# Moving one attention output piece per period by one dense product

## The chip, the cores and the metric

The kernel runs on one core of a Trainium2 chip. The metric is the device time of one execution in microseconds (us), as the median of several runs. TensorE does the matrix products; VectorE, ScalarE and GpSimd empty the PSUM banks, take exponentials and mask; SyncE issues most of the DMA transfers.

## The reference

A transformer block with a pre-norm attention over a sliding window of 256 keys and a dense part with SiLU, for 2048 rows of width 1024, 32 heads of width 32 and a hidden width of 3584:

```python
qkv = layernorm(x) @ wqkv                       # 3 x 32 heads x 32
scores = einsum("bhqd,bhkd->bhqk", q, k) * 32 ** -0.5
mask = (i - j >= 0) & (i - j < 256)
p = softmax(where(mask, scores, -1e9))
h = x + einsum("bhqk,bhkd->bhqd", p, v) @ wo
out = h + silu(layernorm(h) @ w1) @ w2
```

## The kernel before

The 2048 rows are worked in four blocks of 512. TensorE runs one stream of dense products, 128x128 weights against 512 columns, in groups of eight that add up in one PSUM bank: first the q, k and v products of all blocks (lines 252 and 262), then the output projection of the attention (line 283), then the two matrices of the dense part (lines 728 and 756). Three banks (`bank0` to `bank2`) serve the groups in turn; after each group VectorE copies or adds the bank out (lines 254, 264, 285).

Attention is woven into this stream by the class `Attention`. Its counter `seen` counts dense products, and `between` is called ahead of each product: when the counter has reached a number in `pieces` or `visits`, that piece of attention work is put into TensorE's order there. The numbers are written out by hand. `i` counts units of four heads of one block; i = 0 to 7 (block 0) are done with `scores_0`, and the other 24 units in twelve periods of two units each. Period p starts at product t = 256 + 48p and has:

- three score visits, at t + 4, t + 20 and t + 36. A visit (`visit`, line 360) multiplies q and k for 36 to 48 small tiles. Its own tiles go into the four-bank tile `sc`, and, since that is not enough room, others go into the dense bank that is idle, the dense bank of the group just finished ("behind"), and the output bank `bank3`. The products are sorted by column, so that the first 24 of a visit write `sc`, and those for the other banks follow. A product that writes the bank "behind" has to stand after VectorE's copy of that bank. ScalarE then takes the exponentials (lines 315, 321, 322), and GpSimd masks (line 409).
- four output pieces (`attn_piece`), each 24 products of probabilities with v into the output bank `bank3` (line 419), followed by `attn_norm` on VectorE: a reciprocal of the sums (line 430) and a multiply that reads the output bank and writes `obuf` (line 431). Two pieces (heads 0 and 1, then 2 and 3) make a unit; after the second one a transposing DMA of `obuf` is put on the list `late`, which is run, on SyncE's queue, ahead of the next dense group (line 439).

There is one output bank, so a piece must wait until the norm of the piece before has read it, and a visit that uses it must do so too. The first visit of the next period stands at t + 52. Groups of eight start at multiples of eight, so products t + 40 to t + 47 make one group.

Of the kernel before, what the change touches and what calls it, by code (L numbers as in the profile page):

```python
# [47 lines left out]
def kernel(  # L48
# [328 lines left out]
    def scores_0(g, odd):  # L377

        q0 = odd * P
        parts = [  # L380
            (odd, 0, q0, q0 + 320, 0), (odd, 1, q0, q0 + 384, 0),
            (odd + 2, 0, q0 + 256, 448, 320), (odd + 2, 1, q0 + 320, 448, 384),
        ]
        if odd:
            parts = [(a, h, f, min(t, 512), c) for a, h, f, t, c in parts[:2]] + [
                (3, 0, 384, 512, 320), (3, 1, 448, 512, 384), (2, 0, 448, 512, 448), (2, 1, 448, 512, 448)]
        for step in range(0, len(parts), 2):
            for hh in range(4):
                for t, half, qa, qb, col in parts[step:step + 2]:
                    r0 = hh * DH  # L390
                    k0 = t * P + half * 64
                    nc.tensor.matmul(  # L392
                        sc[half * 64:half * 64 + 64, hh, col:col + qb - qa],
                        lhsT=kT[0][r0:r0 + DH, g, k0:k0 + 64],
                        rhs=qT[0][r0:r0 + DH, g, qa:qb],
                        start=True, stop=True, tile_position=(r0, half * 64),
                    )
        e = (ybuf if odd else xbuf)(g)[:, 0:2048].rearrange("p (h q) -> p h q", q=512)
        nc.scalar.activation(out=e[:, :, 0:256], in_=sc[:, :, 0:256], func=ACT.Exp, scale=scale)  # L399
        nc.scalar.activation(out=e[:, :, 320:512], in_=sc[:, :, 256:448], func=ACT.Exp, scale=scale)  # L400
        nc.scalar.activation(out=c_ring[:, (g + 1) % 3, :, 128 + 64 * odd:192 + 64 * odd], in_=sc[:, :, 448:512],
                             func=ACT.Exp, scale=scale)
        select(e[:, :, 0:P], e[:, :, 0:P], True)
        select(e[:, :, 256:384], e[:, :, 320:448], False)
        select(e[:, :, 384:512], e[:, :, 384:512], True)
# [42 lines left out]
    class Attention:  # L448


        def __init__(self):
            self.seen = 0
            self.visits, self.pieces = {}, {}
            for d in range(2 * G):
                self.visits[92 + 10 * d] = lambda d=d: scores_0(d // 2, d % 2)
                self.pieces[(122 + 10 * d, 267, 284)[max(d - 13, 0)]] = (d // 2, d % 2)
            for p in range((NB - 1) * G // 2):
                i, t = G + 2 * p, 256 + 48 * p
                for n in range(3):
                    self.visits[t + 4 + 16 * n] = lambda i=i, n=n: visit(i, n)  # L460
                for n in range(4):
                    self.pieces[t + (41, 45, 59, 76)[n]] = (i + n // 2, n % 2)

        def between(self, kt):
            if self.seen in self.pieces:
# [168 lines left out]
    for g0 in range(0, G, 4):  # L634
        for w in range(2):
            for g in range(g0, g0 + 4):
                run_late()
                n = g0 * 2 + w * 4 + g % 4
# [170 lines left out]
```

## Time and profile before

| what | value |
|---|---|
| median of 3 runs | 690.12 us (689.69 to 690.25) |
| profiled execution | 690.01 us |
| its span, first to last instruction | 688.3 us |
| mean granted TensorE clock | 1.000 |
| TensorE matmul (PE) busy | 674.4 us, 98% |
| TensorE weight load (PEld) busy | 338.1 us, 49% |
| VectorE (DVE) busy | 296.0 us, 43% |
| ScalarE (ACT) busy | 237.8 us, 35% |
| GpSimd (POOL) busy | 155.4 us, 23% |
| attention periods p = 0 to 11 | about 99 to 270 us |

A row of the profile gives an engine, a line of the kernel, an operation with the tile that it writes and the tiles that it reads, and a count; in a timeline the first column is the start and the second the duration, and an idle time of the engine ahead of the row stands in brackets with what ended it. PE rows are matmuls, PEld rows are the weight loads ahead of them. The matmuls are pipelined, so a row's duration reaches beyond the start of the next one, and a few matmul records are missing from the trace; the weight loads are all there.

### The profile page before, as it was taken

The page shows a single profiled execution, that of the slowest core. Times are in us where ns is not written, and L with a number is a line of the kernel's source. Part 1 is how long each engine was busy: PE and PEld are TensorE (multiplying, and loading weights), DVE is VectorE, ACT ScalarE, POOL GpSimd, SP SyncE. Part 2 cuts the span into 40 slices and gives each one's busy share as a digit, 9 for nine tenths or more (in the row PEclk, how much of TensorE's full clock was granted, in tenths as well). Part 3 has the DMA queues.
Part 4 walks back from the last instruction along what each step waited for, and adds up shares of the span by engine and source line. Part 5 has one row for each costly group of instructions (what it writes and reads, how often), then busy time and mean ns, then how long its engine had stood idle before and what let it go on. Part 6 is the DMA issues. An engine that isn't in the chain of part 4 may idle for free.

```text
span 688.3 us, 14482 instructions
## 1 busy us (share of the span) xinstructions
PE 674.4 (98%) x6099; PEld 338.1 (49%) x6200; DVE 296.0 (43%) x616; ACT 237.8 (35%) x412; POOL 155.4 (23%) x247
## 2 busy tenths in 40 slices
PE   9999999999999999999999999999999999999998
PEld 4445555555555555444444444444444444444445
DVE  5287745774444446733316133343233251333111
ACT  7356666666767664023300033300133100233000
POOL 1046656666676665000000000000000000000000
DMA  8823144124522687765023310023300124100110
GB/s 274 260 53 96 21 59 101 26 42 106 174 78 71 199 283 212 157 244 202 1 87 112 84 39 1 0 92 73 81 1 0 31 87 90 39 1 0 31 38 24
DMA packets 77617, 61.50 MB, mean 89 GB/s; under 512 B 52464, under 2 KB 60656, under 8 KB 77552
## 3 DMA queue, kind: packets, MB, share of 16 engines
q1 hardware_dynamic: 77408, 60.31, 31.3%
q8 instruction: 48, 0.79, 0.5%
q10 hardware_dynamic: 144, 0.26, 0.1%
q14 instruction: 17, 0.14, 0.1%
HBM read 39.85 MB, written 8.39 MB: 70 GB/s over the span
## 4 chain that ended last, share of the span: by engine, by line
PE 97%; issue 2%; DMA 1%; DVE 0%; SPq 0%; ACT 0%; ACTq 0%; DVEq 0%
PE hacc L728 16%; PE bank L262 16%; PE hacc L756 15%; PE bank L756 13%; PE bank L728 12%; PE bank L283 8%; PE bank L252 6%; PE bank L419 5%; PE sc L360 2%; PE bank L360 1%; PE bank L547 1%; PE sc L392 1%; DMA r_w<-in_A_wqkv_dram 1%; PE tp L252 1%; ACT r_e L321 0%
## 5 line engine op out<-in xcount | busy, mean ns | idle before, releaser
L409 POOL TENSOR_SCALAR_AFFINE_SELECT r_e<-r_e 128x512 bf16<-128x512 bf16 x240 | 152.5, 643 | 115.3 <-ACT r_e L399 52.4
L756 PEld LDWEIGHTS <-r_a 128*128 128x128 bf16 x952 | 90.9, 98 | 103.0
L728 PEld LDWEIGHTS <-r_w 128*128 128x128 bf16 x896 | 87.7, 98 | 105.7
L756 PE MATMUL hacc<-r_a 128*128 128x512 bf16 (+2 forms) x523 | 103.2, 356 | 0.5
L756 PE MATMUL bank<-r_a 128*128 128x512 bf16 x412 | 91.4, 379 | 0.5
L728 PE MATMUL hacc<-r_e,r_w 128*128 128x512 bf16 x375 | 84.4, 379 | 0.5
L262 PEld LDWEIGHTS <-r_w 128*128 128x128 bf16 x512 | 45.4, 97 | 49.3 <-issue 1.0
L728 PE MATMUL bank<-r_e,r_w 128*128 128x512 bf16 x284 | 63.9, 379 | 0.1
L264 DVE CAST r_a<-bank 128x512 bf16<-128x512 f32 x58 | 40.1, 691 | 53.9 <-PE bank L262 34.3
L262 PE MATMUL bank<-r_t,r_w 128*128 128x512 bf16 x236 | 57.1, 379 | 2.6 <-issue 2.2
L262 PE MATMUL bank<-r_w 128*128 128x512 bf16 x240 | 56.4, 379 | 1.9 <-issue 1.6
L283 PE MATMUL bank<-r_o,r_a 128*128 128x512 bf16 x242 | 56.4, 379 | 1.5 <-issue 1.1
L419 PEld LDWEIGHTS <-r_e 128*128 128x128 bf16 x1440 | 45.6, 96 | 16.8 <-issue 3.2
L321 ACT ACTIVATE r_e<-sc 128x1536 bf16<-128x1536 f32 x36 | 53.4, 1482 | 0.0
L737 ACT ACTIVATE r_n<-bank 128x512 f32<-128x512 f32 x18 | 10.7, 597 | 117.0 <-PE bank L728 117.0
L419 PE MATMUL bank<-r_a,r_e 128*128 128x33 bf16 x1440 | 46.2, 178 | 0.1
L315 ACT ACTIVATE r_e<-bank 128x512 bf16<-128x512 f32 x48 | 26.1, 597 | 45.0 <-PE bank L360 45.0
L737 ACT ACTIVATE r_n<-hacc 128x512 f32<-128x512 f32 x24 | 14.3, 597 | 75.5 <-PE hacc L728 74.3
L771 DVE SCALAR_TENSOR_TENSOR r_t<-bank,r_t 128x512 bf16<-128x512 f32 x15 | 10.3, 684 | 66.6 <-PE bank L756 66.6
L283 PEld LDWEIGHTS <-r_a 128*128 128x128 bf16 x256 | 23.4, 97 | 25.8
L771 DVE SCALAR_TENSOR_TENSOR r_t<-hacc,r_t 128x512 bf16<-128x512 f32 (+2 forms) x19 | 12.0, 632 | 53.1 <-PE hacc L756 53.1
L252 PE MATMUL bank<-r_w,r_t 128*128 128x512 bf16 x118 | 28.9, 379 | 1.1 <-issue 0.8
(100 smaller groups left out, 574.8 us busy)
## 6 DMA issues: line engine op xcount, KB each, us to landing
r_w<-in_B_w_dram SPq DMA_DIRECT2D x8, 896.0 KB, 6.0
r_a<-in_B_w_dram SPq DMA_DIRECT2D x7, 1024.0 KB, 9.8
r_w<-in_A_wqkv_dram SPq DMA_DIRECT2D x4, 1024.0 KB, 8.3
h_dram<-r_t SPq DMA_DIRECT2D x16, 256.0 KB, 2.8
r_t<-h_dram SPq DMA_DIRECT2D x16, 256.0 KB, 2.9
out_dram<-r_t SPq DMA_DIRECT2D x31, 128.0 KB, 1.7
r_e<-h_dram SPq DMA_DIRECT2D x3, 1024.0 KB, 5.8
r_o<-in_A_x_dram SPq DMA_DIRECT2D x11, 256.0 KB, 5.5
```

What stands on the lines that cost most here:

```text
L252: nc.tensor.matmul(acc, lhsT=lnT_b[b % 2][:, kt, j * P:(j + 1) * P], rhs=wv[:, kt, c * 512:(c + 1) * 512], start=(kt == 0), stop=(kt == KT ...
L262: nc.tensor.matmul(acc, lhsT=wqk[:, kt, col0:col0 + P], rhs=lnT_b[b % 2][:, kt, :], start=(kt == 0), stop=(kt == KT - 1))
L264: copy(out=(qT, kT)[which][b][:, g, :], in_=acc)
L283: nc.tensor.matmul(acc, lhsT=qT[b][:, g, j * P:(j + 1) * P], rhs=wo[:, g, c * 512:(c + 1) * 512], start=(g == 0), stop=(g == G - 1))
L315: nc.scalar.activation(out=c_ring[:, lo:hi + 1:hi - lo, h, :], in_=four[bank].rearrange("p (n q) -> p n q", q=256), func=ACT.Exp, scale=scale)
L321: nc.scalar.activation(out=tri_of(e)[:, h0:h1, :, 64:256], in_=tri, func=ACT.Exp, scale=scale)
L409: nc.gpsimd.affine_select(out=dst, in_=src, pattern=[[0, n] for n in dst.shape[1:-1]] + [[sgn, P]], compare_op=ALU.is_ge if upper else ALU ...
L419: nc.tensor.matmul(o_ps[:, qt * 2 + hh, 0:VW], lhsT=chunk_of(i, bank, piece, pair * 2 + hh), rhs=v[:, b * 4 + kt, g * 4 + pair * 2 + hh, : ...
L728: nc.tensor.matmul(acc, lhsT=w1[:, kt, ft * P:(ft + 1) * P], rhs=ln2T[b][:, kt, :], start=(kt == 0), stop=(kt == KT - 1))
L737: nc.scalar.activation(out=th, in_=acc, func=ACT.Tanh, scale=0.5)
L756: nc.tensor.matmul(acc[:, 0:c1 - c0], lhsT=gT[:, ft, j * P:(j + 1) * P], rhs=w2[ft // 4][:, ft % 4, c0:c1], start=(ft == 0), stop=(ft == F ...
L771: nc.vector.scalar_tensor_tensor(out=t_out[j % 2][:, c0:c1], in0=acc[:, 0:c1 - c0], scalar=0.5, in1=t_in[j % 2][:, c0:c1], op0=ALU.mult, o ...
```

## The change

The third visit of a period stands at t + 36, five products ahead of the first output piece at t + 41. The second piece stood at t + 45; it now stands at t + 46, still within the same dense group. Between the two pieces there are then five dense products in place of four, and between the second piece and the next period's first visit at t + 52 six in place of seven. Nothing else differs.

```diff
                 for n in range(4):
-                    self.pieces[t + (41, 45, 59, 76)[n]] = (i + n // 2, n % 2)
+                    self.pieces[t + (41, 46, 59, 76)[n]] = (i + n // 2, n % 2)
```

## The prediction

> **What bounds the kernel now.** I read the page first: its span, the busy shares, and the chain that ended last.
>
> ```profile
> span 688.3 us, 14482 instructions
> PE 674.4 (98%) x6099; PEld 338.1 (49%) x6200; DVE 296.0 (43%) x616; ACT 237.8 (35%) x412; POOL 155.4 (23%) x247
> PE 97%; issue 2%; DMA 1%; DVE 0%; SPq 0%; ACT 0%; ACTq 0%; DVEq 0%
> ```
>
> TensorE is busy 98% of the span and carries 97% of the chain. So time is won only where TensorE stands still or waits, and what is won there moves the end by as much, unless a later wait takes it back. The edit touches twelve places, the second output piece (line 419) of each of the twelve periods. I therefore asked next for the weight loads of that line over the stretch that holds these periods, with what they waited for.
>
> ```profile
> L419 PEld LDWEIGHTS <-r_e x1104: 95/96/98, 101.3 to 269.0; 128*128 128x128 bf16 x184
> its engine sat idle before it (us, times) until:
>   issue: 3.0, 12
> ```
>
> Twelve interruptions, one for each period, 3.0 us in all; the 1104 loads are 46 pieces of 24, and the other 34 (first, third, fourth) show none. Third came the timeline of one period, around the third visit's two pieces. Columns are start, duration, engine, line.
>
> ```profile
> 206.36 0.27 ACT L322 ACTIVATE r_e<-bank 128x128 bf16<-128x128 f32 x1
> 206.39 0.59 PE L262 MATMUL bank<-r_t,r_w 128*128 128x512 bf16 x2
> 206.61 0.86 PEld L419 LDWEIGHTS <-r_e 128*128 128x128 bf16 x24
> 206.82 0.76 PE L419 MATMUL bank<-r_a,r_e 128*128 128x33 bf16 x24
> 207.40 0.55 PEld L262 LDWEIGHTS <-r_w 128*128 128x128 bf16 x4
> 207.42 1.02 PE L262 MATMUL bank<-r_t,r_w 128*128 128x512 bf16 x4
> 207.68 0.21 DVE L430 RECIPROCAL recip<-bank 128x8 f32<-128x8 f32 x1
> 207.93 0.42 DVE L431 TENSOR_TENSOR r_n<-bank,recip 128x256 bf16<-128x256 f32 x1
> 208.07 0.10 PEld L419 LDWEIGHTS <-r_e 128*128 128x128 bf16 x1
> 208.40 0.75 PE L419 MATMUL bank<-r_a,r_e 128*128 128x33 bf16 x24
> 208.40 0.65 PEld L419 LDWEIGHTS <-r_e 128*128 128x128 bf16 x23 [0.24 <-issue]
> 208.98 1.20 PEld L262 LDWEIGHTS <-r_w 128*128 128x128 bf16 x7
> 209.19 0.21 DVE L430 RECIPROCAL recip<-bank 128x8 f32<-128x8 f32 x1 [0.84 <-PE bank L419]
> 209.43 0.42 DVE L431 TENSOR_TENSOR r_n<-bank,recip 128x256 bf16<-128x256 f32 x1
> 209.85 0.69 DVE L264 CAST r_a<-bank 128x512 bf16<-128x512 f32 x1
> 209.92 1.19 SPq L439 DMA_TRANSPOSE r_a<-r_n  x1
> 210.60 0.57 PEld L360 LDWEIGHTS <-r_a 32*64 32x64 bf16 x48 [0.42 <-issue]
> 210.60 0.43 PE L360 MATMUL sc<-r_a 32*64 32x320 bf16 x24
> 210.85 0.47 PE L360 MATMUL bank<-r_a 32*64 32x128 bf16 x24
> 211.32 1.57 ACT L315 ACTIVATE r_e<-bank 128x512 bf16<-128x512 f32 x3 [2.30 <-PE bank L360]
> ```
>
> Both pieces write the one output bank. The second may not write before VectorE's norm of the first (lines 430 and 431) has read it. The norm ends at 207.93 + 0.42 = 208.35 and the second piece's first matmul starts at 208.40, 0.05 later, while its first weights had been in since 208.17. That the norm is the releaser is borne out by the one period where it is late:
>
> ```profile
> 117.80 0.10 PEld L419 LDWEIGHTS <-r_e 128*128 128x128 bf16 x1
> 117.80 0.42 DVE L431 TENSOR_TENSOR r_n<-bank,recip 128x256 bf16<-128x256 f32 x1
> 118.28 0.65 PEld L419 LDWEIGHTS <-r_e 128*128 128x128 bf16 x23 [0.38 <-issue]
> 118.86 1.20 PEld L252 LDWEIGHTS <-r_w 128*128 128x128 bf16 x7
> 119.73 0.69 DVE L254 CAST r_a<-bank 128x512 bf16<-128x512 f32 x1
> 120.48 0.57 PEld L360 LDWEIGHTS <-r_a 32*64 32x64 bf16 x48 [0.42 <-issue]
> ```
>
> Here it ends at 118.22, and the piece goes on at 118.28, after 0.38 of idle instead of 0.24.
>
> **The change part by part.** No instruction is added, removed or resized; 24 matmuls with their weight loads, one reciprocal and one multiply per period come one dense product later in TensorE's order.
>
> *What goes.* A dense product takes 0.215 us: the row at 206.39 holds two in 0.59, that at 207.42 four in 1.02, so two more cost 0.43. Without a wait the second piece's first matmul would start one product after its first weight load, at 208.07 + 0.215 = 208.285; it starts 0.115 later. The whole slot says the same: from the piece's first weight load to the next product's it is 208.98 - 208.07 = 0.91, against 207.40 - 206.61 = 0.79 for the first piece, 0.12 more. In the late period the slot is 118.86 - 117.80 = 1.06, 0.27 more by these rounded rows. The group row makes the ordinary period general: 3.0 less the late one's 0.38, over eleven, is 0.24, the very idle of the period shown. So the stalls are worth 11 x 0.115 + 0.26 = 1.5 us.
>
> With one product more, the ordinary piece's natural start is 208.285 + 0.215 = 208.50, past the release at 208.40 by 0.10. A release that comes shortly ahead costs nothing: the first piece's bank is freed by ScalarE at 206.36 + 0.27 = 206.63, it starts at 206.82, and its slot is the 0.79. So the wait goes entirely in eleven periods. In the late one the natural start is 117.80 + 0.43 = 118.23 and the release 118.28: 0.05 stays. Gain 1.45 us. From below: if the piece's new place in its group of eight cost 10 ns each, and the 3.0 us stands rounded, 1.3; from above: by idle alone, 3.0 - 12 x 0.12 (the idle behind a first weight load that needs no wait: 0.215 less its 0.10) = 1.56, less the 0.05, 1.5.
>
> *What is late next.* The piece itself begins 0.10 later (208.50 for 208.40), and so does everything VectorE does behind it: reciprocal from 209.29, norm until 209.95, and queued behind the norm the cast of the finished dense group, 209.95 to 210.64. The dense products behind the piece, and with them the next period's first visit (line 360), come 0.115 earlier: the visit at 210.49, and its 24 products into the chained banks from 210.74 on. One of these banks is that which the cast empties, and in the order in which the code sorts the visit's products it is the fifth of the 24, about 210.75. The cast's release is 210.64 + 0.05 = 210.69. In the trace of before this cover is 210.86 - 210.59 = 0.27; it shrinks to some 0.06, and does not go. I cost it at nothing. The late period has as much: cast until 120.42, release 120.47, and its visit at 120.27, its bank products from 120.52. In the last period no visit follows.
>
> The output bank, which the same visit writes too, is free at 209.95 + 0.05, 0.7 ahead. SyncE's transpose of the normed tile waits for the norm: 0.10 later, its data are for the last projection, and it is issued at the same group boundary in SyncE's order, so no load is overtaken. ScalarE waits 2.30 for the visit at 211.32 and moves with it; GpSimd follows ScalarE.
>
> *Sum.* The profiled execution took 690.01 us with a span of 688.3; less 1.45 it is 688.56. The median of the three runs is 690.12, 0.11 above; carried over, 688.67, that is 0.21% less.
>
> **The rivals.** *The cover is too thin by the refill.* [...]
>
> ```profile
> 60.41 0.10 PEld L419 LDWEIGHTS <-r_e 128*128 128x128 bf16 x1
> 60.73 0.50 PEld L419 LDWEIGHTS <-r_e 128*128 128x128 bf16 x17 [0.22 <-issue]
> 61.26 0.32 PEld L392 LDWEIGHTS <-r_a 32*64 32x64 bf16 x24
> ```
>
> From 60.73 until about 61.48 (61.26 + 0.32 less a load of 0.10) 17 + 24 weight loads with their matmuls came: at most 18 ns a pair, and less if the array was the limit. At 18 ns the 20 pairs from the waiting product on would need until 210.69 + 0.36 = 211.05; their natural last load is 210.60 + 0.57 - 0.10 - 0.115 = 210.955. Loss 0.095 in eleven periods, 1.05 us: 689.7 at worst, nothing at 13 ns or below. I take 689.4 for this case. For it: the cover of 0.06. Against: visits show weight loads a few ns apart, and the 18 ns is a ceiling.
>
> [...]
>
> *Slower: the visit needs the cast at its head.* If what is held up by the cast were the visit's first product, not its 29th (one wait for the whole visit, or a queue that must be full before it starts), the release at 210.69 would stand against 210.49: 0.20 lost for 0.115 won, and a refill of 48 pairs at 18 ns, 0.86 for the visit's 0.50 or so, another 0.36. That is 0.445 net in ten periods and 0.35 in the late one, less 0.115 in the last: 4.7 us, 694.8; without the refill still 0.8, 690.9. It decides from the point where the release is needed ahead of 210.69, so anything that wants it 0.06 before its bank product tips toward it. For it: today the cast ends at 210.54, 0.06 ahead of the visit, so the trace of before would hide such a need. Against: the gap ahead of a visit (0.42) is the same in the late period, and the first 24 products write only the score tile.
>
> *Nothing moves.* The 0.12 could belong to a second piece as such, wherever it stands: 690.1. Against: the 0.38 that follows the late norm.
>
> **How the numbers follow.** A measurement of this kernel can tell about 0.2%, 1.4 us, from no change, so the forecast lies almost on that bound. The stall goes as worked out: 0.76. Of this 0.58 I put beyond 0.2% and 0.18 within, since the gain of 1.3 to 1.5 straddles 1.38, and the higher of its terms rest on the better rows. Thin cover: 0.08, within. Nothing moves: 0.05, within. Slower at the head: 0.11, of it 0.09 with the refill, over 0.2% slower, and 0.02 within. Faster 0.58, same 0.33, slower 0.09. The predicted time is 688.67. The range goes down to 688.2 (the 1.5, and the 0.43 by which the lowest run of before lies below its median) and up to 689.6, which takes in the thin cover's 689.4 and leaves out no change and the slower case, 0.16 together.
>
> **What would show it.** Right: the interruptions of line 419's weight loads in this stretch fall from twelve to one, of about 0.17; the second piece's slot falls to 0.79 or 0.80; reciprocal and norm of that piece stand one product later against the piece before; the gap ahead of the next first visit stays 0.42 and its 48 loads stay 0.57; the dense line's count between the two pieces is five, not four. Thin cover: the visit's loads stretch beyond 0.57 by up to 0.1. Slower: the 0.42 becomes 0.6 or more in eleven periods. Nothing moves: an idle of 0.24 stays ahead of the piece's second load. The prediction is wrong if TensorE's time ahead of the last projection does not shrink by 1.3 to 1.5 us, or if that gain is gone again by the end.

## The result

| kernel | median | runs | ratio to before, 95% interval |
|---|---|---|---|
| before | 689.99 us | 13 (689.68 to 690.45) | |
| changed | 688.79 us | 13 (688.25 to 690.04) | 0.9981 [0.9973, 0.9989] |

The change makes the kernel 1.20 us faster by the medians, 0.17%; the ratio in the table says 0.19%, and its interval ends below 1, so a gain is there, though a small one. The forecast was 688.67 in a range of 688.2 to 689.6. On the bound of 0.2% that the prediction set for itself the result falls just within, as its text said it might; it had given the larger chance, 0.58, to the other side.

The profiled execution of the changed kernel took 689.66 us with a span of 688.0. That is only 0.35 below the 690.01 of before, so its stages have to be read apart. First the page, then the weight loads of line 419 over the periods, with what they waited for:

```profile
span 688.0 us, 14583 instructions
PE 682.9 (99%) x6200; PEld 338.0 (49%) x6200; DVE 295.0 (43%) x616; ACT 237.8 (35%) x412; POOL 155.5 (23%) x247
PE 98%; DMA 1%; SPq 0%; DVE 0%; issue 0%
```

```profile
L419 PEld LDWEIGHTS <-r_e x1122: 95/96/98, 98.3 to 268.9; 128*128 128x128 bf16 x187
its engine sat idle before it (us, times) until:
  issue: 0.2, 1
```

Twelve interruptions have become one, and 3.0 us of idle 0.2. That is not 2.8 us won: in every piece, waiting or not, TensorE's weight loads stand still for 0.12 us behind the first one (in each of the 62 pieces of this trace without a wait; at 208.38 the first load takes 0.10 and the second starts at 208.60), which this view does not count, and that part stays. (The PE busy time is higher because this trace lacks no matmul records, 6200 for 6099.) The timeline of the same period as in the prediction:

```profile
207.49 0.77 PEld L262 LDWEIGHTS <-r_w 128*128 128x128 bf16 x5
207.52 1.24 PE L262 MATMUL bank<-r_t,r_w 128*128 128x512 bf16 x5
207.77 0.21 DVE L430 RECIPROCAL recip<-bank 128x8 f32<-128x8 f32 x1
208.02 0.42 DVE L431 TENSOR_TENSOR r_n<-bank,recip 128x256 bf16<-128x256 f32 x1
208.38 0.87 PEld L419 LDWEIGHTS <-r_e 128*128 128x128 bf16 x24
208.59 0.76 PE L419 MATMUL bank<-r_a,r_e 128*128 128x33 bf16 x24
209.17 0.98 PEld L262 LDWEIGHTS <-r_w 128*128 128x128 bf16 x6
209.39 0.21 DVE L430 RECIPROCAL recip<-bank 128x8 f32<-128x8 f32 x1 [0.94 <-PE bank L419]
209.63 0.42 DVE L431 TENSOR_TENSOR r_n<-bank,recip 128x256 bf16<-128x256 f32 x1
209.97 0.68 DVE L264 CAST r_a<-bank 128x512 bf16<-128x512 f32 x1
210.58 0.57 PEld L360 LDWEIGHTS <-r_a 32*64 32x64 bf16 x48 [0.42 <-issue]
210.83 0.47 PE L360 MATMUL bank<-r_a 32*64 32x128 bf16 x24
```

Five products stand between the pieces. The norm ends at 208.44, the piece starts at 208.59, its 24 weight loads run through in one group, and its slot is 209.17 - 208.38 = 0.79. The visit behind keeps its gap of 0.42 and its 0.57. The late period:

```profile
118.89 0.10 PEld L419 LDWEIGHTS <-r_e 128*128 128x128 bf16 x1
119.16 0.65 PEld L419 LDWEIGHTS <-r_e 128*128 128x128 bf16 x23 [0.17 <-issue]
119.73 0.98 PEld L252 LDWEIGHTS <-r_w 128*128 128x128 bf16 x6
```

Its slot is 0.84, 0.05 above the others; that is the one interruption left.

Where, then, are the other 1.1 us of this execution? At the start and at the end of the periods, neither of which the change touches. TensorE's third value product (line 547) started 0.62 us later, since it waited for value weights from DRAM. First the row of before, then that of the changed kernel:

```profile
6.65 5.93 PE L547 MATMUL bank<-r_w 128*128 128x512 bf16 x25 [0.28 <-DMA r_w<-in_A_wqkv_dram]
7.27 6.07 PE L547 MATMUL bank<-r_w 128*128 128x512 bf16 x26 [0.95 <-DMA r_w<-in_A_wqkv_dram]
```

And the last period's third visit was held up:

```profile
264.87 0.65 PEld L360 LDWEIGHTS <-r_a 32*64 32x64 bf16 x36 [0.42 <-issue]
265.58 0.76 PEld L283 LDWEIGHTS <-r_a 128*128 128x128 bf16 x5
```

By the time of the first score product of block 0 this execution was 0.99 us behind that of before (41.57 for 40.58, the first weight load of line 392), all of it lost in the first 22 us. The visit's slot is 265.58 - 264.87 = 0.71 where it was 0.58. Between the first load of line 392 and the first of line 728, the stretch that holds all the periods, the trace of before has 257.78 us and this one 256.44: 1.34 less, which is 1.47 less 0.13 at that visit; the slots of the twelve pieces account for 1.45 of the 1.47. So the gain is there in full, and what a single run shows of it depends on the start and on that visit. The experiments look into both.

### The profile page after: what moved, and what is told of

Same layout as the page of the kernel before. It is cut to its first block, busy times and chain, and to the rows that moved or that the text cites. A ratio compares the mean times of both kernels' runs of the same rounds, so it can differ in the third digit from the quotient of the medians.

```text
span 688.0 us, 14583 instructions
## 1 busy us (share of the span) xinstructions
PE 682.9 (99%) x6200; PEld 338.0 (49%) x6200; DVE 295.0 (43%) x616; ACT 237.8 (35%) x412; POOL 155.5 (23%) x247
## 4 chain that ended last, share of the span: by engine, by line
PE 98%; DMA 1%; SPq 0%; DVE 0%; issue 0%
PE bank L262 17%; PE hacc L728 16%; PE hacc L756 15%; PE bank L756 13%; PE bank L728 12%; PE bank L283 8%; PE bank L252 7%; PE bank L419 5%; PE sc L360 2%; DMA r_w<-in_A_wqkv_dram 1%; PE bank L360 1%; PE sc L392 1%; PE tp L252 1%; PE bank L547 0%; PE tp L499 0%; SPq L150 0%
## 5 line engine op out<-in xcount | busy, mean ns | idle before, releaser
L262 PE MATMUL bank<-r_t,r_w 128*128 128x512 bf16 x256 | 61.3, 379 | 0.0
L262 PE MATMUL bank<-r_w 128*128 128x512 bf16 x256 | 59.4, 379 | 0.1
L283 PE MATMUL bank<-r_o,r_a 128*128 128x512 bf16 x256 | 58.9, 379 | 0.0
L252 PE MATMUL bank<-r_w,r_t 128*128 128x512 bf16 x128 | 30.5, 380 | 0.0
```

What stands on the lines that cost most here:

```text
L252: nc.tensor.matmul(acc, lhsT=lnT_b[b % 2][:, kt, j * P:(j + 1) * P], rhs=wv[:, kt, c * 512:(c + 1) * 512], start=(kt == 0), stop=(kt == KT ...
L262: nc.tensor.matmul(acc, lhsT=wqk[:, kt, col0:col0 + P], rhs=lnT_b[b % 2][:, kt, :], start=(kt == 0), stop=(kt == KT - 1))
L283: nc.tensor.matmul(acc, lhsT=qT[b][:, g, j * P:(j + 1) * P], rhs=wo[:, g, c * 512:(c + 1) * 512], start=(g == 0), stop=(g == G - 1))
```

## The experiments

Theory: the second piece waits for the norm of the first; each product between them hides 0.215 us of it; and the visit behind needs VectorE's cast only at its 29th product. Rivals: the visit needs the cast at its head; the 0.12 us belong to any second piece; the change makes a later wait.

**One product more: t + 47.**

```diff
-                    self.pieces[t + (41, 46, 59, 76)[n]] = (i + n // 2, n % 2)
+                    self.pieces[t + (41, 47, 59, 76)[n]] = (i + n // 2, n % 2)
```

> Own theory (the second piece waits for the norm, and the next visit needs the bank behind only at its 29th product): no wait left at the piece, its slot 0.795 us in all twelve periods. The norm of the second piece ends 0.215 us later than at t + 46, so the cast's release comes some 0.16 us after the visit's 29th product would start. The visit's weight loads stretch from 0.57 to about 0.73 us in eleven periods, 1.75 us lost for 1.50 won against before: 690.2 us, up to 691.5 if the refill behind the wait takes 18 ns a pair. The gap ahead of the visit stays 0.42. Rival (the visit needs the cast at its head): the gap grows by about 0.42 us to 0.84 in eleven periods, 693 us or more. Rival (the cover is never used): 688.5 us.

Measured: 689.32 us, ratio 0.9985 [0.9976, 0.9994]. The profile has no interruption of line 419 left. The same period in its timeline:

```profile
208.56 0.42 DVE L431 TENSOR_TENSOR r_n<-bank,recip 128x256 bf16<-128x256 f32 x1
208.90 0.68 DVE L264 CAST r_a<-bank 128x512 bf16<-128x512 f32 x1
209.30 0.59 PEld L360 LDWEIGHTS <-r_a 32*64 32x64 bf16 x48 [0.42 <-issue]
209.54 0.50 PE L360 MATMUL bank<-r_a 32*64 32x128 bf16 x24
209.97 0.98 PEld L262 LDWEIGHTS <-r_w 128*128 128x128 bf16 x6
```

The cast ends at 209.58, its release reaches TensorE at about 209.63, 0.33 after the visit has started; this is an estimate by the 0.05 that lay between the norm's end and the piece's start in the trace of before (208.35 and 208.40). The gap ahead of the visit is still 0.42, so the visit does not need the cast at its head: that rival falls. The cover is used up now, as the theory said, but the price was far off. The 29th product, due at about 209.555 (its bank products begin at 209.54), is by that 0.08 late, not 0.16; and the visit's slot (from its first weight load to the next dense one) grows only from 0.65 to 0.67 or 0.68. Over eleven periods that is 0.3 us, not 1.75. Two reasons are in these rows. The cast starts at 208.90, 0.08 ahead of the end of the multiply before it on the same engine; the prediction had them end to end. And a visit has slack behind its 29th product: the 20 products left follow one another so closely after the release that most of the delay is made up. They start between 209.64 and about 209.83 (209.54 + 0.50 less one product's 0.21), 0.19 us in all and 10 ns apart on the mean; in the changed kernel, where nothing holds them up, they take from 210.84 to 211.09 (210.83 + 0.47 - 0.21), 0.25 us. At the stretch from line 392 to line 728 this kernel has 256.60 us, 1.18 below before: 1.5 from the pieces, 0.3 given back. The profiled execution, 688.37 us, is the lowest of the eleven. Their median lies 0.60 above that of the second series of the changed kernel (below, timed in the same comparison), where the stretches differ by 0.28; no profile shows where the other executions lost the rest.

**One product less: t + 44.**

```diff
-                    self.pieces[t + (41, 46, 59, 76)[n]] = (i + n // 2, n % 2)
+                    self.pieces[t + (41, 44, 59, 76)[n]] = (i + n // 2, n % 2)
```

> Own theory: one dense product less hides 0.215 us less of the norm, in every period: idle ahead of the piece's second weight load 0.45 us in place of 0.24 (0.60 in the late period), 12 x 0.215 = 2.6 us slower than before, 692.6 us. Rival (the 0.12 us belongs to a second piece as such, wherever it stands): 690.0 us, idle 0.24 as before.

Measured: 692.80 us, ratio 1.0043 [1.0030, 1.0055]; 2.58 above the median of before, against 12 x 0.215 = 2.58. The weight loads of line 419 between 98 and 267 us:

```profile
L419 PEld LDWEIGHTS <-r_e x1074: 95/96/98, 98.0 to 266.4; 128*128 128x128 bf16 x179
its engine sat idle before it (us, times) until:
  issue: 5.1, 11
```

The eleven periods in this window should give 10 x 0.45 + 0.60 = 5.1, and do. The 0.12 us of before are therefore what four products leave uncovered, and no property of a second piece.

**A shorter norm, the piece left at t + 45.** Half of the first piece's output is left out in each period:

```diff
+        w = DH // 2 if i >= G and i % 2 == 0 and pair == 0 else DH
...
-            in0=o_ps[:, :, 0:DH].rearrange("p (t h) d -> p t h d", h=2),
+            in0=o_ps[:, :, 0:w].rearrange("p (t h) d -> p t h d", h=2),
```

> The second piece stays at t + 45; the multiply of the first piece's norm in each period covers half of its columns, so half of that piece's output is left out. Own theory: the multiply takes about 0.29 us for 0.42, the release comes at 208.27 where the piece could start at 208.285, the wait goes in eleven periods and some 0.13 us stays in the late one: 1.4 us faster than before, 688.6 us. The next visit's cover stays what it was before. Rival (the wait is not for the norm): 690.0 us, idle 0.24.

Measured: 689.07 us, ratio 0.9984 [0.9972, 0.9997]. The same period:

```profile
206.93 0.29 DVE L432 TENSOR_TENSOR r_n<-bank,recip 128x128 bf16<-128x128 f32 x1
207.07 0.86 PEld L419 LDWEIGHTS <-r_e 128*128 128x128 bf16 x24
207.87 1.20 PEld L262 LDWEIGHTS <-r_w 128*128 128x128 bf16 x7
```

The multiply takes 0.29, the slot is 0.80 with only four products between the pieces, and 0.3 us in one place is all that is left of the idle. The releaser is the norm: shortening it does what moving the piece does. The median gain is 1.15 and not 1.4. In this profile, of an execution near the median (689.10), the last period's third visit lost 0.66 us; whether the other executions lost as much is not shown. Without that the stretch from line 392 to line 728 is 256.41 us, 1.37 below before.

**The changed kernel again, and a third time; and the kernel before again.**

> The changed kernel once more, for the spread of its runs. Own theory: the second piece's slot is 0.795 us in eleven periods and 0.84 in the late one in every profile, so 1.45 us below before from the piece alone; what a single run shows beyond that comes from the loads of the first 20 us: lowest run about 688.3, median 688.5 to 688.9. Rival (the change makes something later wait, in every run): the wait ahead of the last period's third visit, 0.13 us in the first profile, is there again and the first 20 us are alike.

> The changed kernel a third time, for its profile. If the late wait belongs to the change: again 0.1 to 0.2 us. If it is chance: anything from 0 to 0.7 us. The second piece's slots as in the other two profiles.

> The kernel before once more, for its profile: does the last period's wait for a store to the scratch rows in DRAM, which the changed kernel shows with 0.13 to 0.17 us, occur without the change too? If it is chance of the transfers: some 0 to 0.7 us at the last period's third visit or at the fourth piece of the period before, as at t + 44 (0.67). If the change causes it: nothing there, as in the first profile of before. The second piece's idle is 0.24 in eleven periods either way.

The second series of the changed kernel: 688.72 us (688.40 to 689.02), ratio 0.9979 [0.9970, 0.9988], 1.50 below the median of before in that comparison; the third, one run, 688.62. The slots of the second piece are the same in all three profiles. The late wait is no work of the change: it was 0.13 and 0.17 in two profiles of the changed kernel and nothing in the third, and the kernel before shows it too, with nothing in its first profile and 0.43 in its second. The rows are of that second profile, of SyncE, VectorE and TensorE:

```profile
254.81 0.38 SPq L623 DMA_DIRECT2D r_a<-h_dram  x1
256.53 0.84 SPq L288 DMA_DIRECT2D h_dram<-r_t  x1
```

```profile
263.81 0.69 DVE L285 TENSOR_TENSOR r_t<-bank,r_a 128x512 bf16<-128x512 f32 x1 [3.58 <-DMA h_dram<-r_t]
```

```profile
265.05 0.34 PEld L360 LDWEIGHTS <-r_a 32*64 32x64 bf16 x27 [0.42 <-issue]
265.73 0.27 PEld L360 LDWEIGHTS <-r_a 32*64 32x64 bf16 x9 [0.33 <-issue]
```

These rows give the chain. The load of the first block's rows for the second norm (L623, 1 MB) goes ahead of a store of projected rows (L288) in SyncE's queue. VectorE's add (L285) that reuses that store's tile waits for it until 263.81, 7.3 us after the store was issued. The next add is late by that, and so is the bank that the visit needs from its 28th weight load on. The other profiles agree (last table of this section). In all eight that have the load at this place, VectorE stands idle ahead of this add for longer than the 1.78 us that it takes where no transfer is waited for, and the longer it stands, the more TensorE loses: nothing up to 2.77, 0.13 to 0.17 at 3.17 and 3.28, 0.43 at 3.58, 0.66 and 0.67 at 3.81 and 3.82. With the piece at t + 45 the idle is 2.12 and 3.58, at t + 46 it is 2.63 to 3.28, so it shows no tie to the piece's place.

**The load later.** In both kernels, the load two groups later and the norm's steps with it:

```diff
-        if n == 9:
+        if n == 11:
...
-            if steps and n >= 13:
+            if steps and n >= 15:
```

> The changed kernel, with the load of the first block's rows for the second norm issued after the twelfth group of the output projection, not the tenth, and that norm's steps begun two groups later. Theory: that load waits in SyncE's queue for the stores of the same rows, and the stores and loads queued behind it come late, so VectorE's add at the end of the last period waits for a store and TensorE for VectorE. Two groups later the stores have landed: the wait in the last period is gone in the profile, the runs spread less, median 0.1 to 0.3 us below that of t + 46 alone, about 688.5 us. Rival (the wait comes from the load on the transfers in this stretch, whoever is first in the queue): as t + 46 alone, 688.7, the wait still there or moved.

> The kernel before with the same later load. Against load_later_46 it gives the price of the second piece's place with that wait out of the way: own theory 1.45 us slower than load_later_46, 689.9 to 690.0 us. Rival (part of the 1.45 us is given back in the output projection by the transfers): the difference between the two is 1.2 us or less, as between the medians of the first comparison.

Measured, in one comparison (median of before 690.37): with the piece at t + 46 688.36 us (688.17 to 688.61), ratio 0.9966 [0.9953, 0.9978]; with it at t + 45 690.08, ratio 0.9995 [0.9986, 1.0004]. The two medians differ by 1.72 us and the stretches by 1.49, so the rival that part of the gain is given back among the transfers falls. In the profile at t + 46 the add no longer waits for a transfer, and the visit is whole:

```profile
260.45 0.69 DVE L285 TENSOR_TENSOR r_t<-bank,r_a 128x512 bf16<-128x512 f32 x1 [1.78 <-ACT r_e L321]
```

```profile
263.48 0.52 PEld L360 LDWEIGHTS <-r_a 32*64 32x64 bf16 x36 [0.42 <-issue]
264.06 0.76 PEld L283 LDWEIGHTS <-r_a 128*128 128x128 bf16 x5
```

At t + 45 the idle ahead of the add is the same 1.78. By its median the version at t + 46 is the fastest here. How much of it is the later load alone is not settled by the times: at t + 45 the interval holds no change, and at t + 46 the kernels with and without it were timed in different comparisons, but for one run without it, 688.62. The profiles show what it takes away, a wait of TensorE of 0 to 0.67 us.

The stretch from the first weight load of line 392 to the first of line 728, start of the last less start of the first, and the late wait in it (what the last period's third visit, or in the second profile of the changed kernel the piece before it, took beyond its usual slot); the last column is VectorE's idle ahead of the add described above. In the kernel with half a norm line 728 is one further down.

| profile | stretch, us | late wait | stretch without it | VectorE idle |
|---|---|---|---|---|
| before | 257.78 | 0 | 257.78 | 2.12 |
| before again | 258.21 | 0.43 | 257.78 | 3.58 |
| t + 45, load later | 257.83 | 0 | 257.83 | 1.78 |
| changed | 256.44 | 0.13 | 256.31 | 3.28 |
| changed again | 256.49 | 0.17 | 256.32 | 3.17 |
| changed, third | 256.33 | 0 | 256.33 | 2.63 |
| t + 46, load later | 256.34 | 0 | 256.34 | 1.78 |
| half norm, t + 45 | 257.07 | 0.66 | 256.41 | 3.81 |
| t + 47 | 256.60 | 0 | 256.60 | 2.77 |
| t + 44 | 261.07 | 0.67 | 260.40 | 3.82 |

Behind it all ten take 389.92 to 389.94 us. Ahead of it they differ by up to 1.45 us (40.12 to 41.57) with the same code.

## Why the prediction was right, point by point

*The stall and its size.* Shown. The wait was for the norm (t + 44 lengthens it by a product, a shorter norm removes it), it was 0.11 to 0.12 in eleven periods and 0.26 in one, and 1.45 us of it went. The table's stretches without the late wait are 257.80 for the piece at t + 45 and 256.325 for t + 46 as means: 1.47 apart.

*No wait left in eleven periods, 0.05 in the late one.* Shown: 0.79 and 0.84.

*The place in the group costs nothing.* The bound of 10 ns each, the author's own estimate, was not needed: 0.79, as for the first piece.

*What is late next.* The direction held, the size was off. The prediction left the cast a cover of 0.06 before the 29th product. In the profile after, the release is at 209.97 + 0.68 + 0.05 = 210.70 and the bank products begin at 210.83: a cover of about 0.14. The step that failed is the one that put the cast behind the norm, end to end: 209.97 is 0.08 ahead of 210.05. It was too cautious, and cost nothing. In the trace of before the cast does start at 209.85, where the norm ends, but the norm need not have been what held it there. TensorE's last product of the group that the cast empties, the third behind the piece, ended only 0.04 earlier, at 209.81, and by the 0.08 the norm alone would have let the cast begin at 209.77:

```profile
209.43 0.38 PE L262 MATMUL bank<-r_t,r_w 128*128 128x512 bf16 x1
```

With the piece one product later this group ends 0.18 ahead of the cast (its last product is at 209.41, so 209.41 + 0.38 = 209.79), and VectorE alone sets its start.

*Thin cover, 18 ns a pair.* At t + 46 nothing of it is seen: the visit's 48 loads take 0.57 as before. It was priced by a ceiling, the 41 pairs in 0.75 us that came behind an earlier wait of 0.22 at 60.73, and that lies far from what was measured: at t + 47 the cover is gone, the products come 10 ns apart on the mean, and the whole price is 0.03 a period. At 18 ns the 20 pairs from the release at 209.63 would need until 209.99, and their last load is due at 209.77 (209.30 + 0.57 - 0.10): 0.22. Nor did the wait make the products behind it slower to start: 0.19 us for these 20, for 0.25 where nothing held them up.

*Slower at the head.* Ruled out twice: after the change the release comes at 210.70, 0.12 after the visit's start at 210.58, and the gap is 0.42; at t + 47 it comes 0.33 after it.

*Nothing moves.* Ruled out by t + 44 and by the shorter norm.

*The median.* 1.20 in the first comparison and 1.50 in the second, around the 1.45 that the stages show. The prediction counted neither the 1.45 us by which the first 22 us differ between the profiles nor the late wait for a store; both occur without the change. That its range held them is luck: it had been drawn to the lowest run of before and to the thin cover.

## What to carry to other kernels

When a hand-written order puts two users of one buffer a few products apart, take the stall from the idle ahead of the second user, less the idle that a user shows there that did not wait, group it over all places, and see whether it is less than one product: then one step of the order removes it. What follows on the other side is a cover that shrinks, at most by as much as the piece moved and the engine gained together (here from 0.27 to 0.14, for 0.10 and 0.115). Write down at which instruction of the next burst it is needed: here a burst of small products took a release that came 0.08 late in its middle for 0.03. When a gain is near the spread of the runs, compare a stretch between two fixed instructions of the trace rather than the whole time.

## What the runs showed of the hardware that was not expected

Where nothing else held it, VectorE started a cast 0.08 us ahead of the profiled end of the multiply before it, on other banks (209.97 for 210.05; 208.90 for 208.98). Behind a release in the middle of a visit TensorE took up its small products 10 ns apart on the mean (20 in 0.19 us, with the release put 0.05 behind the cast's end, for 0.25 without a wait), and so made up more than half of a delay of 0.08: the visit's slot grew by 0.02 to 0.03. And a store of 256 KB that followed a 1 MB load on the same queue held VectorE up until 7.3 us after its issue, enough to reach TensorE through two VectorE adds, for 0.43 us.
